# A fused attention and swish kernel: batch 2's queries turned by DMA, two block products alternated, one norm moved

## Chip, cores and metric

The kernel runs on one core of one Trainium2 chip. The metric is the device time of one execution in microseconds (us); lower is better. A change of some 0.2% of it (0.55 us) is about the smallest that the measurement tells from none.

## What is computed

The reference has two stages. The first is an attention without a score matrix: the queries get a softmax over the head's 64 columns, the keys a softmax over the sequence, and each head's 64x64 product of keys and values is applied to the queries. The second is a two-layer network with a swish.

```python
# q, k, v: (batch 8, heads 8, seq 576, dim 64)
q_s = softmax(q, axis=-1)
k_s = softmax(k, axis=2)
kv  = einsum('bhsd,bhse->bhde', k_s, v)
x   = einsum('bhsd,bhde->bhse', q_s, kv)      # then to (4608 tokens, 512)
h   = x @ w_in                                # 512 -> 2048
g   = h / (1 + exp(-beta * h))
out = g @ w_out                               # 2048 -> 512
```

## The kernel before

The 4608 tokens are worked off in nine slabs of 512. Slab t (0 to 7) holds the first 512 rows of batch t's sequence; slab 8 holds the last 64 rows of all eight batches, the "remainder".

**A slab.** Each slab has two passes. Pass 1 forms h transposed, 16 tiles of 128 features by 512 tokens, from WIN and XT (four matmuls of 512 columns a tile, L377). ScalarE applies the swish (L628), VectorE scales by 1/beta (`scale_g`, L651), and the result is GT. Pass 2 multiplies GT by WOUT. In slab 0 it is the plain product (`pass2_group`). In slabs 1 to 8 it is `pass2_fast`, which cuts the product into 2x2 blocks and needs seven block products in place of eight. Each block product is 16 matmuls of 256 columns (L728), eight blocks i for two halves u. The first, into bank s, multiplies GS1 (a sum of two quarters of GT) by WSUM; the second, into bank z5, multiplies GS2 (another sum) by WOUT. The sums are made on VectorE during pass 1, in pieces: blocks 0 to 3, then 4 and 5, then 6, then 7 (L682 `g_sum1`, L687 `g_sum2`). Block 7 can be summed only after the slab's last tile has gone through ScalarE and `scale_g`. When both products are done VectorE copies bank s to TS (L792) and subtracts bank z5 from it (L795), later bank z2 (L801). Bank z5 is then written again by the fourth product. Two differences of GT (`g_diff`, L694) are made on VectorE and used by the last two products.

**Attention.** Batch t+1's attention is laid between the matmuls of slab t and of the next pass 1. ScalarE takes exponentials (L300, and L312 for the key remainder). A norm (`norm_main`) is a sum over 64 columns (L331) and a reciprocal (L332) on VectorE, and a product (L333) on VectorE or POOL, as its last argument says. The normed queries EQ are transposed to QT in one of two ways: on TensorE with an identity (`t_steps`, L375, evacuated to QT at L395), or by a DMA transpose [...], issued from SP (`turn`, L484; `norm_turn` is a norm on POOL and a `turn`). `kv_steps` form keys times values (EK and VB, remainder EKR and VR), VectorE scales and masks them into KVD (L439, L419), and `out_step` multiplies KVD by QT (four per batch, L377) and evacuates to XT (L457). Batches 0, 1 and 2 are transposed on TensorE, batches 3 to 7 by DMA.

**Order.** All order is written by hand. Each engine runs its own list in the order in which the program adds operations, with semaphore waits derived from reads, writes and PSUM banks. In the slabs, `tick` counts matmuls (64 slots for pass 1, 32/56 of a slot for each of the 112 matmuls of pass 2) and releases the items of `todo` when their slot is reached. `hooks` of pass 2 release loads, exponentials, casts and norms at eight points between the products. All loads, stores and DMA transposes of the slabs are issued from SP's queue in program order. Batch b uses buffer b % 2 of QF, KF, VF, EQ and QT.

In slab 1, hook 0 releases the exponentials and V casts of batch 2 and the load of batch 4; hooks 2 and 3 release batch 2's two norms on POOL. `attn_late(2)` places four transposes at a time, then keys times values, then the four `out_step`s. In slab 2, `attn_late(3)` places keys times values at slots 97 to 105 and two `out_step`s at 117 to 120.

Of the kernel before, what the change touches and what calls it, by code (L numbers as in the profile page):

```python
# [154 lines left out]
def bass_efficient_attn_shen__then__act_swish_beta_kernel(  # L155
# [12 lines left out]
    with ExitStack() as es:  # L168
# [340 lines left out]
        def attn_late(b):  # L509
            x = []  # L510
            for hp in range(NHP):
                x += out_step(b, hp, MB, ACTE if hp % 2 else DVE)
            k01, k23 = kv_steps(b, (0, 1)), kv_steps(b, (2, 3))
            if b == 2:
                s = spread(t_steps(b, (0, 1), MB, ACTE), 104, 107) + spread(k01, 107, 110)
                s += spread(k23, 110, 113) + [(113.5, lambda: g_diff(1))] + spread(x[0:2], 114, 116)
                s += spread(t_steps(b, (2, 3), MB, ACTE), 116.5, 119)
                return s + spread(x[2:4], 123, 126)
            if b == 3:
                s = spread(k01, 97, 101) + spread(k23, 101, 105) + [(105, lambda: g_diff(1))]  # L520
                return s + spread(x[0:2], 117, 120)
            s = spread(k01, 92, 96) + spread(k23, 96, 99.8) + [(100, lambda: g_diff(1))]
            return s + spread(x, 107, 123)

        def spread(steps, lo, hi):
            return [(lo + (hi - lo) * k / len(steps), s) for k, s in enumerate(steps)]
# [165 lines left out]
        def g_diff(fh):  # L692
            f, th = NG * fh, 1 - fh
            add(DVE, lambda e: e.tensor_tensor(gv(f, th, NG), gv(f, th, NG), gv(f, 1 - th, NG),  # L694
                                               ALU.subtract),
                r=gk(f, 0, NG) + gk(f, 1, NG), w=gk(f, th, NG), war=True)
# [20 lines left out]
        def pass2_fast(t, tick, hooks):  # L717
            s, z5, z2 = HB[hrot[0] % 3], OB[0], OB[1]
            z2s = (OB[1], MB[0]) if t == NSLAB - 1 else (z2, z2)

            def prod(bk, lhs, lk, rhs, rk, first, end=False):
                two = bk == z2 and z2s[0] != z2s[1]
                for i, u in ([(i, u) for u in range(2) for i in range(NG)] if two and end else
                             [(i, u) for i in range(NG) for u in range(2)]):
                    l, r_ = lhs(i, u), rhs(i)
                    st = first and i == 0 and (u == 0 or two)
                    b_ = z2s[u] if two else bk
                    add(PE, lambda e, l=l, r_=r_, st=st, u=u, i=i, b_=b_: e.matmul(  # L728
                        PS[b_][:, 256 * u:256 * u + 256], l, r_, start=st, stop=end and i == NG - 1,
                        skip_group_check=True),  # L730
                        r=lk(i) + rk(i), w=[("ps", b_)], bank=[b_])
                    tick(32.0 / 56)

            def gt(f0, th):
                return (lambda i, u: GT[:, f0 + i, 256 * th + 128 * u:256 * th + 128 * u + 128],
                        lambda i: [("gt", f0 + i, th)])

            def gs2(th):
                return (lambda i, u: GS2[:, i, 256 * th + 128 * u:256 * th + 128 * u + 128],
                        lambda i: [("gs2", i)])  # L740

            def wo(fh, dh):
                return (lambda i: WOUT[:, NG * fh + i, 256 * dh:256 * dh + 256],
                        lambda i: [("wout", NG * fh + i, dh)])

            def wsum(n):
                return lambda i: WSUM[n][:, i, :], lambda i: [("ws", n, i)]

            def out(th, dh):
                return (O2S[t % 2][:, 2 * th:2 * th + 2, 256 * dh:256 * dh + 256],  # L750
                        [("o2", t % 2, 2 * th + u, dh) for u in range(2)])

            def bank3(bk):
                return PS[bk][:, :].rearrange("p (a b) -> p a b", b=256)

            def halves(bk):
                if bk == z2 and z2s[0] != z2s[1]:
                    return [(z2s[0], 0, 1), (z2s[1], 1, 2)]
                return [(bk, 0, 2)]

            def copy(bk, th, dh, eng):
                o, w = out(th, dh)
                for b_, u0, u1 in halves(bk):
                    add(eng, lambda e, b_=b_, u0=u0, u1=u1: (  # L764
                        e.copy if eng == ACTE else e.tensor_copy)(
                        o[:, u0:u1, :], bank3(b_)[:, u0:u1, :]),
                        r=[("ps", b_)], w=w[u0:u1], bank=[b_])
                if t == 8:
                    store8(th, dh)

            def last(bk, th, dh):
                o, w = out(th, dh)
                ts = TS[:, :].rearrange("p (a b) -> p a b", b=256)
                h = halves(bk)
                for b_, u0, u1 in h:
                    add(DVE, lambda e, b_=b_, u0=u0, u1=u1: e.tensor_tensor(  # L776
                        o[:, u0:u1, :], ts[:, u0:u1, :], bank3(b_)[:, u0:u1, :], ALU.add),
                        r=["ts", ("ps", b_)], w=w[u0:u1], bank=[b_])
                    if t == 8 and len(h) == 2:
                        store8(th, dh, u0)  # L780
                if t == 8 and len(h) == 1:
                    store8(th, dh)

            def at(n):
                for f in hooks.get(n, ()):
                    f()

            at(0)
            prod(s, lambda i, u: GS1[:, i, 128 * u:128 * u + 128], lambda i: [("gs1", i)],
                 *wsum(0), True, True)  # L790
            prod(z5, *gs2(0), *wo(1, 1), True)
            add(DVE, lambda e: e.tensor_copy(TS[:, :], PS[s][:, :]), r=[("ps", s)], w=["ts"],  # L792
                bank=[s])
            at(1)
            add(DVE, lambda e: e.tensor_tensor(TS[:, :], TS[:, :], PS[z5][:, :], ALU.subtract),  # L795
                r=["ts", ("ps", z5)], w=["ts"], bank=[z5])
            at(2)
            prod(z2, *gs2(1), *wo(0, 0), True)
            for b_, u0, u1 in halves(z2):
                c = slice(256 * u0, 256 * u1)  # L800
                add(DVE, lambda e, b_=b_, c=c: e.tensor_tensor(  # L801
                    TS[:, c], TS[:, c], PS[b_][:, c], ALU.subtract),
                    r=["ts", ("ps", b_)], w=["ts"], bank=[b_])
            if t > 3:
                g_diff(0)
                g_diff(1)
            at(3)
            prod(z5, *gt(0, 0), *wo(0, 1), False)
            copy(z5, 0, 1, ACTE)
            at(4)  # L810
            prod(z2, *gt(NG, 1), *wo(1, 0), False)
            copy(z2, 1, 0, ACTE)
            at(5)
            prod(z5, *gt(0, 1), *wsum(1), False, True)
            last(z5, 1, 1)
            at(6)
            prod(z2, *gt(NG, 0), *wsum(2), False, True)
            last(z2, 0, 0)
            at(7)
# [15 lines left out]
        def steps(fn, *a):  # L835
            return lambda: go(fn(*a))

        for t in range(NSLAB):
# [12 lines left out]
                todo += [(2, steps(out_step, 0, 3, HEAD, DVE))]  # L851
            elif t < 4:
                todo = attn_late(t + 1)
                if t == 3:
                    todo += [(1, steps(out_step, 3, 2, MB, ACTE)), (2.5, steps(out_step, 3, 3)),
                             (4, one(norm_turn, 4, 2))]
                if t == 1:
                    todo += [(1, steps(out_step, 1, 2, (3,), ACTE)),
                             (3, steps(kv_steps, 1, (3,), (7,))),
                             (6, steps(out_step, 1, 3, (7,), DVE)),  # L860
                             (6.1, one(w_diff, 0)), (6.2, one(w_diff, 1))]
            elif t < 7:
                todo = attn(t + 1)
                if t > 3:
                    todo += spread(outr_steps(2 * t - 5), *((72, 88), (40, 56), (60, 76))[t - 4])
            elif t == 7:
                todo = spread(outr_steps(1), 32, 48)
# [31 lines left out]
            if t == 0:  # L899
# [6 lines left out]
                w_sum(0, 0, 4)  # L906
                w_sum(2, 0, 4)
                norm_main(1, 0, 1, DVE)
                norm_main(1, 1, 1, POOL)
                cast_vr_s(1)  # L910
                w_sum(0, 4, 4)
                w_sum(2, 4, 4)
# [29 lines left out]
            if t == 1:  # L942
                on(0, exps, 2)
                on(0, casts, 2)
                on(0, load, 4)
                on(2, norm_main, 2, 0, 2, POOL)
                on(3, norm_main, 2, 2, 2, POOL)
                on(3, g_diff, 0)
            elif t == 2:
                on(0, exps, 3)  # L950
                on(2, norm_turn, 3, 0)
# [67 lines left out]
```

The softmax here doesn't subtract the row's maximum and nothing guards it: scores larger than these inputs give would overflow.

## Time and profile before

| | us |
|---|---|
| median of 3 runs (276.8 to 277.07) | 276.98 |
| the profiled execution | 277.22 |
| its span in the profile | 275.2 |
| PE busy / idle in the span | 269.1 / 6.1 |
| VectorE (DVE) busy | 193.8 |
| ScalarE (ACT) busy | 183.1 |
| GpSimd (POOL) busy | 64.0 |
| slab 1, first block matmul to that of slab 2 | 61.20 to 91.11 |
| slab 2, the same | 91.11 to 119.29 |

PE is TensorE's matmul stream and PEld its weight loads, which may run ahead. SPq is SP issuing a DMA. A row of the timeline gives start, duration, engine, line, operation, output and inputs, shape, and a count where neighbours were merged; a bracket at its end gives how long that engine had been idle just before and what ended the idle time. A DMA's landing is counted from its issue. The granted TensorE clock is at full speed through the whole span.

### The profile page before, as it was taken

The numbers are of one execution on the slowest core, as the hardware profiler recorded it, in microseconds if no ns is written. First come the engines' busy times: TensorE is split into PE (matmuls) and PEld (weight loads), VectorE is DVE, ScalarE is ACT, GpSimd is POOL, SyncE is SP. The second block draws the span as 40 slices with busy tenths as digits, with TensorE's granted clock in tenths as the row PEclk, the third lists the DMA queues.
The fourth block names the chain that finished last, engine by engine and source line by source line (L and its number), as shares of the span: only waits on it lengthen the run. The fifth ranks groups of instructions, "written<-read, shape, count | busy, mean of one in ns | idle before, by whom it ended". The sixth has DMA issues, their size and how long they took to land.

```text
span 275.2 us, 4707 instructions
## 1 busy us (share of the span) xinstructions
PE 269.1 (98%) x1841; PEld 167.9 (61%) x1841; DVE 193.8 (70%) x414; ACT 183.1 (67%) x286; POOL 64.0 (23%) x82
## 2 busy tenths in 40 slices
PE   8999999999999999999999999999999999999994
PEld 2544444448754785478656875587558745874583
DVE  4954586787758799878778776978497549625862
ACT  4887558789478966896778937893773477018610
POOL 2780030007421089100810570036000100000000
PEclk9999999999999999999999999999999999999999
DMA  7999999989991029930499999103600130012005
GB/s 215 314 205 207 229 331 349 281 258 376 357 299 60 0 42 289 322 117 0 80 276 292 337 335 194 58 4 76 210 2 0 21 152 0 2 54 99 2 0 153
DMA packets 57254, 45.39 MB, mean 165 GB/s; under 512 B 26497, under 2 KB 56209, under 8 KB 56209
## 3 DMA queue, kind: packets, MB, share of 16 engines
q1 hardware_dynamic: 52368, 40.38, 51.3%
q0 software_dynamic: 4240, 4.19, 9.3%
q10 hardware_dynamic: 624, 0.53, 0.6%
q8 instruction: 14, 0.23, 0.4%
q14 instruction: 8, 0.06, 0.1%
HBM read 36.71 MB, written 9.44 MB: 168 GB/s over the span
## 4 chain that ended last, share of the span: by engine, by line
PE 83%; DMA 8%; POOL 4%; DVE 2%; issue 1%; ACT 0%; SPq 0%; POOLq 0%
PE PS L377 49%; PE PS L728 33%; DMA WOUT<-in_moe_w_out_dram 5%; DMA QF<-in_q_dram 3%; POOL EQ L333 2%; POOL WIN L552 1%; POOL VB L348 1%; PE PS L375 1%; DVE QS L331 1%; POOL VR L362 0%; DVE XT L457 0%; ACT GT L628 0%; DVE EQ L333 0%; DVE QI L332 0%; ACT EQ L300 0%
## 5 line engine op out<-in xcount | busy, mean ns | idle before, releaser
L377 PE MATMUL PS<-XT,WIN 128*128 128x512 bf16 x576 | 131.0, 379 | 0.1
L628 ACT ACTIVATE GT<-PS,BETA 128x512 bf16<-128x512 f32 x144 | 95.2, 690 | 39.5 <-PE PS L377 38.9
L377 PEld LDWEIGHTS PS<-XT,WIN 128*128 128x128 bf16 x576 | 53.6, 98 | 61.1 <-DVE XT L457 0.6
L651 DVE TENSOR_SCALAR GT<-GT,RB 128x512 bf16<-128x512 bf16 x144 | 52.1, 381 | 37.1 <-ACT GT L628 36.4
L333 POOL TENSOR_TENSOR EQ<-EQ,QI 128x1024 bf16<-128x1024 bf16 (+1 forms) x14 | 26.9, 1921 | 66.9 <-DVE QI L332 66.2
L728 PE MATMUL PS<-WOUT,GT 128*128 128x256 bf16 x256 | 33.6, 273 | 0.0
L728 PE MATMUL PS<-WSUM,GT 128*128 128x256 bf16 x256 | 31.9, 273 | 0.1
L728 PE MATMUL PS<-WOUT,GS 128*128 128x256 bf16 x256 | 30.4, 273 | 0.0
L728 PEld LDWEIGHTS PS<-WSUM,GT 128*128 128x128 bf16 x256 | 24.9, 98 | 4.0 <-issue 0.2
L728 PEld LDWEIGHTS PS<-WOUT,GT 128*128 128x128 bf16 x256 | 25.0, 98 | 3.4
L728 PEld LDWEIGHTS PS<-WOUT,GS 128*128 128x128 bf16 x256 | 24.6, 98 | 3.4
L764 ACT COPY O2S<-PS 128x512 f32<-128x512 f32 (+1 forms) x17 | 9.4, 561 | 24.1 <-PE PS L728 22.7
L300 ACT ACTIVATE EQ<-QF 128x512 bf16<-128x512 f32 x32 | 18.0, 621 | 7.2 <-DMA QF<-in_q_dram 7.2
L687 DVE TENSOR_TENSOR GS<-GT 128x512 bf16<-128x512 bf16 (+2 forms) x32 | 21.9, 685 | 0.0
L348 POOL CAST VB<-VF 128x512 bf16<-128x512 f32 x25 | 15.7, 629 | 25.8 <-DVE GS L687 14.8
L377 PE MATMUL PS<-VB,EK 128*128 128x129 bf16 x128 | 20.6, 220 | 0.0
L331 DVE TENSOR_REDUCE QS<-EQ 128x16 f32<-128x1024 bf16 (+1 forms) x20 | 19.8, 991 | 0.8 <-ACT EQ L300 0.8
L694 DVE TENSOR_TENSOR GT<-GT 128x2048 bf16<-128x2048 bf16 x16 | 19.7, 1259 | 0.0
L300 ACT ACTIVATE EK<-KF 128x512 bf16<-128x512 f32 x32 | 18.1, 621 | 0.0
L776 DVE TENSOR_TENSOR O2S<-TS,PS 128x512 f32<-128x512 f32 (+1 forms) x17 | 10.7, 644 | 8.8 <-PE PS L728 8.8
L457 ACT CAST XT<-PS 128x512 bf16<-128x512 f32 x18 | 10.4, 582 | 9.4 <-PE PS L377 9.4
L728 PE MATMUL PS<-WSUM,GS 128*128 128x256 bf16 x128 | 16.4, 273 | 0.0
(78 smaller groups left out, 241.8 us busy)
## 6 DMA issues: line engine op xcount, KB each, us to landing
out_dram<-O2S SPq DMA_DIRECT2D x8, 1024.0 KB, 5.4
QF<-in_q_dram SPq DMA_DIRECT2D x6, 1024.0 KB, 7.5
KF<-in_k_dram SPq DMA_DIRECT2D x6, 1024.0 KB, 9.1
VF<-in_v_dram SPq DMA_DIRECT2D x6, 1024.0 KB, 12.0
KF<-in_k_dram SPq DMA_DIRECT2D x8, 256.0 KB, 5.5
VF<-in_v_dram SPq DMA_DIRECT2D x8, 256.0 KB, 5.5
WOUT<-in_moe_w_out_dram POOLq DMA_DIRECT2D x4, 512.0 KB, 16.4
WIN<-in_moe_w_in_dram POOLq DMA_DIRECT2D x3, 512.0 KB, 9.3
```

The lines of the kernel that those rows point to most:

```text
L300: add(ACTE, lambda e, o=o, a=a: e.activation(o, a, ACT.Exp), r=[(name + "f", i, hp)], w=[("e" + name, i, hp)])
L331: add(DVE, lambda e: e.tensor_reduce(s_, a, AX.X, ALU.add), r=ks, w=[("qs", i, hp0)])
L333: add(eng, lambda e: e.tensor_tensor(a, a, vb, ALU.mult), r=ks + [("qi", i, hp0)], w=ks)
L348: add(eng, lambda e: (e.copy if eng == ACTE else e.tensor_copy)(o, a), r=[("vf", i, hp), ("vone", i)], w=[("vb", i, hp)], after=after)
L377: add(PE, lambda e: e.matmul(o, l, r_, start=start, stop=stop), r=r, w=w, bank=[bk])
L457: add(eng, lambda e: (e.copy if eng == ACTE else e.tensor_copy)(XT[i][:, hp, :], PS[bk][:, :]), r=[("ps", bk)], w=[("xt", i, hp)], bank=[bk])
L628: add(ACTE, lambda e: e.activation(GT[:, f, :], PS[bk][:, :], ACT.Silu, scale=BETA[:, f:f + 1]), r=[("ps", bk), "beta"], w=[("gt", f, 0), ...
L651: add(DVE, lambda e: e.tensor_scalar(GT[:, f, :], GT[:, f, :], RB[:, f:f + 1], None, ALU.mult), r=k + ["rb"], w=k)
L687: add(DVE, lambda e: e.tensor_tensor(GS2[:, i:i + n, :], GT[:, i:i + n, :], GT[:, i + NG:i + NG + n, :], ALU.add), r=[k_ for f in (i, i + ...
L694: add(DVE, lambda e: e.tensor_tensor(gv(f, th, NG), gv(f, th, NG), gv(f, 1 - th, NG), ALU.subtract), r=gk(f, 0, NG) + gk(f, 1, NG), w=gk(f ...
L728: add(PE, lambda e, l=l, r_=r_, st=st, u=u, i=i, b_=b_: e.matmul(PS[b_][:, 256 * u:256 * u + 256], l, r_, start=st, stop=end and i == NG - ...
L776: add(DVE, lambda e, b_=b_, u0=u0, u1=u1: e.tensor_tensor(o[:, u0:u1, :], ts[:, u0:u1, :], bank3(b_)[:, u0:u1, :], ALU.add), r=["ts", ("ps ...
```

## The change

Four edits stand in the diff. The two block products are cut in two: blocks 0 to 5 of the first, blocks 0 to 5 of the second, then blocks 6 and 7 of the first, blocks 6 and 7 of the second (in all of slabs 1 to 8). Batch 2 is treated as batch 3 is: `norm_turn` in place of a norm and `t_steps`, its first two `out_step`s late in slab 1, its last two in pass 1 of slab 2. The load of batch 4 goes from hook 0 of slab 1 to hook 3, behind the two turns on SP's queue. The product of batch 1's second norm goes from POOL to VectorE.

```diff
@@ attn_late @@
-            if b == 2:
-                s = spread(t_steps(b, (0, 1), MB, ACTE), 104, 107) + spread(k01, 107, 110)
-                s += spread(k23, 110, 113) + [(113.5, lambda: g_diff(1))] + spread(x[0:2], 114, 116)
-                s += spread(t_steps(b, (2, 3), MB, ACTE), 116.5, 119)
-                return s + spread(x[2:4], 123, 126)
-            if b == 3:
+            if b < 4:
                 s = spread(k01, 97, 101) + spread(k23, 101, 105) + [(105, lambda: g_diff(1))]
                 return s + spread(x[0:2], 117, 120)
@@ pass2_fast @@
-            def prod(bk, lhs, lk, rhs, rk, first, end=False):
+            def prod(bk, lhs, lk, rhs, rk, first, end=False, part=range(NG)):
                 two = bk == z2 and z2s[0] != z2s[1]
-                for i, u in ([(i, u) for u in range(2) for i in range(NG)] if two and end else
-                             [(i, u) for i in range(NG) for u in range(2)]):
+                for i, u in ([(i, u) for u in range(2) for i in part] if two and end else
+                             [(i, u) for i in part for u in range(2)]):
...
             at(0)
-            prod(s, lambda i, u: GS1[:, i, 128 * u:128 * u + 128], lambda i: [("gs1", i)],
-                 *wsum(0), True, True)
-            prod(z5, *gs2(0), *wo(1, 1), True)
+            def prod_s(part):
+                prod(s, lambda i, u: GS1[:, i, 128 * u:128 * u + 128], lambda i: [("gs1", i)],
+                     *wsum(0), True, True, part)
+
+            prod_s(range(0, 6))
+            prod(z5, *gs2(0), *wo(1, 1), True, False, range(0, 6))
+            prod_s(range(6, NG))
+            prod(z5, *gs2(0), *wo(1, 1), True, False, range(6, NG))
             add(DVE, lambda e: e.tensor_copy(TS[:, :], PS[s][:, :]), r=[("ps", s)], w=["ts"],
                 bank=[s])
@@ the slabs @@
             elif t < 4:
                 todo = attn_late(t + 1)
+                if t > 1:
+                    todo += [(1, steps(out_step, t, 2, MB, ACTE)), (2.5, steps(out_step, t, 3))]
                 if t == 3:
-                    todo += [(1, steps(out_step, 3, 2, MB, ACTE)), (2.5, steps(out_step, 3, 3)),
-                             (4, one(norm_turn, 4, 2))]
+                    todo += [(4, one(norm_turn, 4, 2))]
...
                 norm_main(1, 0, 1, DVE)
-                norm_main(1, 1, 1, POOL)
+                norm_main(1, 1, 1, DVE)
                 cast_vr_s(1)
...
             if t == 1:
                 on(0, exps, 2)
                 on(0, casts, 2)
-                on(0, load, 4)
-                on(2, norm_main, 2, 0, 2, POOL)
-                on(3, norm_main, 2, 2, 2, POOL)
+                on(2, norm_turn, 2, 0)
+                on(3, norm_turn, 2, 2)
                 on(3, g_diff, 0)
+                on(3, load, 4)
```

## The prediction

> **What bounds the kernel now.** I read the page first. TensorE is busy 269.1 of 275.2 us (98%), and the chain of work that ended last is 83% PE. So only two things count: matmul work that disappears, and stretches in which PE waits. The list of waits, cut to PE's weight loads (PEld), says where it waits (columns: total us, times, longest):
>
> ```profile
> PEld PS L728 <- DVE GS L682: 1.7, 7, 0.2
> PEld PS L375 <- POOL EQ L333: 1.4, 2, 1.0
> PEld PS L377 <- ACT QT L395: 0.6, 2, 0.3
> PEld PS L377 <- DMA QT<-EQ: 0.2, 1, 0.2
> ```
>
> Each part of the change has its row. In seven of the eight slabs the block products L728 wait for a block sum GS; in slab 6 they don't, since eight small remainder matmuls stand between the first blocks there. Twice a PE transpose (L375) waits for a norm on POOL. Then the timeline of slab 1 (the first of the eight, t = 1) around its output product; columns are start, duration, engine, operation, count, and in brackets the idle time ahead:
>
> ```profile
> 61.20 2.05 PE L728 MATMUL PS<-WSUM,GS 128*128 128x256 bf16 x16
> 62.51 0.29 DVE L682 TENSOR_TENSOR GS<-GT 128x256 bf16<-128x256 bf16 x1
> 62.85 0.11 PEld L728 LDWEIGHTS PS<-WSUM,GS 128*128 128x128 bf16 x2 [0.25 <-DVE GS L682]
> 63.09 3.66 PE L728 MATMUL PS<-WOUT,GS 128*128 128x256 bf16 x32
> 67.49 4.74 POOL L333 TENSOR_TENSOR EQ<-EQ,QI 128x1024 bf16<-128x1024 bf16 x2
> 69.44 0.11 PEld L375 LDWEIGHTS PS<-IDB,EQ 128*128 128x128 bf16 x2 [0.47 <-POOL EQ L333]
> ```
>
> The reader is to see that the eighth block of the first product is there only at 62.80, while its weights could go at 62.60; and that the first transposes hang on POOL's norm. Next the same place in slab 2, which already has DMA transposes and is my template for slab 1 after the change:
>
> ```profile
> 97.20 4.75 POOL L333 TENSOR_TENSOR EQ<-EQ,QI 128x1024 bf16<-128x1024 bf16 x2 [13.68 <-DVE QI L332]
> 99.13 4.08 SPq L484 DMA_TRANSPOSE QT<-EQ  x2
> 102.54 0.38 PE L377 MATMUL PS<-QT,KVD 128*128 128x512 bf16 x1
> 105.22 0.10 PEld L377 LDWEIGHTS PS<-QT,KVD 128*128 128x128 bf16 x1 [0.19 <-DMA QT<-EQ]
> 105.26 0.38 PE L377 MATMUL PS<-QT,KVD 128*128 128x512 bf16 x1
> ```
>
> Here the second DMA transpose lands just in time: the weights of the third QT product wait 0.19 us for it. Last, the end of slab 0:
>
> ```profile
> 37.36 2.09 DVE L706 TENSOR_TENSOR WSUM<-WOUT 128x1024 bf16<-128x1024 bf16 x2
> 37.60 1.31 POOL L333 TENSOR_TENSOR EQ<-EQ,QI 128x512 bf16<-128x512 bf16 x1 [17.20 <-DVE QI L332]
> 38.96 0.23 PEld L375 LDWEIGHTS PS<-IDB,EQ 128*128 128x128 bf16 x4 [0.98 <-POOL EQ L333]
> 39.38 0.67 DVE L331 TENSOR_REDUCE QS<-EQ 128x8 f32<-128x512 bf16 x1
> 41.07 0.23 PEld L375 LDWEIGHTS PS<-IDB,EQ 128*128 128x128 bf16 x4 [0.48 <-DVE EQ L333]
> ```
>
> **What the Trainium skill says.** (1) "TensorE: Matmul & The Clock Gate", section "Architectural detail": PE may pull weight loads ahead of matmuls in flight. So an idle PEld is not a stopped matmul stream, and the trace agrees: PEld idles 0.25 us, but the first product takes 63.09 - 61.20 = 1.89 us from first matmul to the next product's first, and 16 matmuls at the pace of the next 32 (66.58 - 63.09 = 3.49, 0.109 each) would take 1.745. The stall is 0.145, not 0.25. (2) "SBUF — State Buffer", "Who interferes with whom": a VectorE operation with two SBUF inputs contends with a GpSimd operation that reads SBUF. The trace agrees: the pair of L706 at 37.36 beside POOL's norm takes 2.09 us, the same pair at 32.82 with POOL idle 1.29. (3) "DMA: Bandwidth & Descriptors", "Queues, rings and completion order": each DMA engine consumes a queue's descriptors in ring order. The trace agrees: transposes issued onto a quiet queue land in 3.0 to 3.3 us (99.13: 3.1; the second of that pair 3.2), the one at 109.03 behind three 1 MB loads issued from 103.25 took 7.4, the slowest of all 7.9.
>
> I count from each slab's first block matmul, T0: 61.20, 91.11, 119.29, 148.60, 177.24, 205.51, 232.81, 258.99.
>
> **Part 1, alternation.** No instruction is added or removed. Blocks 6 and 7 of product one now come behind 24 matmuls, 24 x 0.109 = 2.6 us after T0. The last sum (GS1) ends at 62.80 = T0 + 1.6 and the GS2 one at 63.14 = T0 + 1.9; blocks 4 and 5 of GS2, needed at 1.3, ended at 60.28. So the 0.145 goes in each slab that has it. What is late next? Product one now ends four matmuls before product two. VectorE's copy L792 (0.69) starts at about T0 + 3.2, so the subtraction L795 starts at about T0 + 3.9. Before, it started at 94.95 = T0 + 3.84. VectorE does not get earlier, only PE does. PE wants L795's bank again after 48 matmuls, T0 + 5.2, and L795 ends near 4.6: 0.6 to spare. In slabs 3 to 8 nothing on PE follows VectorE closely (the difference g_diff(0) in slab 3 ends at 126.69 = T0 + 7.4, wanted after 80 matmuls and 20 of attention, past 8.7). Gain in slabs 3, 4, 5, 7 and 8: 5 x 0.145 = 0.72. In slab 2 the norm hangs on VectorE behind L795, so the second transpose lands at the same time or 0.05 later, and PE waits for it: gain 0.145 less 0.15 to 0.2, call it 0. Slab 1 is in part 2.
>
> **Part 2, batch 2 by DMA (slab 1).** Removed: 16 PE transposes at about 0.055 us (two of them add 0.11 to the 0.11 of the block matmul beside them: 69.57, 69.79), 0.88 in all; two evacuations of 1.01 on ACT, hidden; and waits of weight loads for the norm, the banks and the evacuation (0.47, 0.16, 0.23, 0.26). The changed order of PE instructions in slab 1 is the same as in slab 2, so I don't add these up: I take slab 2's length, 119.29 - 91.11 = 28.18, in place of slab 1's 91.11 - 61.20 = 29.91, and correct it. Both lengths hold four QT products. Corrections: (a) POOL starts its norms at T0 + 6.29 in slab 1 (it casts V first, to 67.41), at T0 + 6.09 in slab 2; both pairs take the same 4.75. So the second transpose is issued at 72.25 and lands at 75.45 = T0 + 14.25, where slab 2's third QT product ran at 105.26 = T0 + 14.15. That costs 0.1, with the hand-over up to 0.2. (b) ACT's exponential of the K remainder ends at 68.19 = T0 + 7.0; the first remainder matmul, at 98.14 = T0 + 7.03 in slab 2, comes 0.145 earlier now: a wait of about 0.2, which the later wait (a) absorbs. (c) The first transpose is issued at about 69.43, behind the store issued at 58.89 that took 12.0 us, so until 70.9. Quiet, it lands at 72.5; behind that store I allow up to 73. PE wants it at about T0 + 11.45 = 72.65, and the second at least 2.7 us later, 75.35 to 75.7. Again nearly absorbed; I put 0.05 on it. Slab 1 becomes 28.18 + 0.1 to 0.4; I take 28.4. Gain 1.5 (1.3 to 1.65).
>
> The DMA moved too: batch 4's three loads and four remainders stand behind both turns on SP's queue. The first is issued at about 73.6 instead of 65.62. Their issue up to the store's end of landing took 65.62 to 84.8; the same 19 us from 73.6 ends near 92.5. They are needed from 99.43 (ACT's exponential of batch 4), and slab 2's turns come at about 97.5: hidden, by 5 us. Without that cover slab 2 would wait like the 7.4 us case.
>
> **Part 3, batch 1's second norm on VectorE.** POOL's 1.31 becomes 0.69 (the same L333 at 34.98). PE's transposes start at about 38.2 instead of 38.96. But VectorE runs without idle from 36.52 to 42.57: its two L706 now come 0.74 later, at 38.1, and without POOL beside them take 1.29, so the next reduction starts at 39.3 instead of 39.38. PE, after 8 matmuls, waits for that third norm until about 41.0 as before. The stall moves; gain 0 to 0.1. The ends: 0.5 gained (PE's own wait) if the third norm came early enough, 0.7 lost if the L706 stay at 2.09. I take 0.
>
> **Sum.** 1.5 + 0.72 + 0 + 0 = 2.2. Against the profiled run: 277.22 - 2.2 = 275.0. The median of the runs shown is 0.24 below that run, so 276.98 - 2.2 = 274.8.
>
> **Rivals.** (A) The landings don't bind: slab 1 reaches 28.03 (gain 1.88), slab 2 keeps 0.145, slab 0 gives 0.5: with the 0.72, 3.25 in all, 273.7. For it: 0.1 us decides each; against: the 0.19 already waited in slab 2. (B) The alternation's gain is swallowed by VectorE's later subtraction, or the first transpose lands 1 us late behind the store: 0.72 to 1 less, about 275.7. Against the first speaks the 0.6 to spare. (C) Slower: the first turn stands in a full queue. At 7.9 us it lands at 77.3, the first QT product is 4.7 late, the third runs at 80.0 instead of 75.45, and 4.6 lost against 2.2 gained ends at 279.4. It decides from a landing 5.5 us after issue, where the slip reaches 2.2. For it: DMA runs at 350 GB/s until the store lands; against: only 1.5 us of that store is left at 69.4, and the loads now stand behind.
>
> **Chances.** Forecast 0.63 (its own range 274.3 to 275.3), A 0.12, B 0.17, C 0.05, something unseen that leaves it unchanged 0.03. The range 273.7 to 275.8 takes in A and most of B. 0.2% (0.55 us) is about what a measurement can tell from no change.
>
> **What would show it.** The row L728 <- DVE GS gone; first to second product without a gap; slab 1 about 28.4 long, slab 2 28.2, slab 3 29.15; PE waiting for QT's DMA in slabs 1 and 2 by 0.1 to 0.4; L706's second pair at 1.3 and PE's stall in slab 0 now ahead of the third transposes. A QT wait over 1 us in slab 1, a new wait on L795's bank, or a first turn landing after 75 would prove me wrong.

## The result, and the profile after

| | before | changed kernel |
|---|---|---|
| median of 6 runs | 277.01 us | 274.92 us |
| lowest and highest | 276.8, 277.12 | 274.59, 275.83 |
| the profiled execution, its span | 277.22, 275.2 us | 274.92, 273.1 us |

The ratio is 0.9929, with a 95% interval of 0.9914 to 0.9943: 2.1 us, or 0.7%, faster. The forecast was 274.8 us. The sum was nearly met, in part by luck: slabs 0 and 1 gained 0.2 us more than was written for them, and slab 2 lost 0.37. The wider spread (1.24 us between lowest and highest, 0.32 before) was not foreseen at all.

From the list of PE's weight-load waits in the changed kernel (total us, times, longest):

```profile
PEld PS L375 <- DVE EQ L333: 3.0, 6, 1.1
PEld PS L377 <- DMA QT<-EQ: 0.9, 3, 0.5
PEld PS L375 <- POOL EQ L333: 0.6, 1, 0.6
PEld PS L377 <- ACT EKR L312: 0.2, 1, 0.2
PEld PS L377 <- DMA QTR<-EQR: 0.2, 1, 0.2
```

The row of the block products waiting for GS is gone. Of the first row's 3.0 us, 1.6 stand at the end of slab 0; the rest, and the row of POOL, lie in batch 0's attention at the start, whose last transposes come at 12.18 in both kernels. The wait for QT's DMA has grown from 0.2 us once to 0.9 in three places. At the end stands a row that the kernel before did not have: a wait for QTR, the remainder's DMA transpose. It is short in this execution, but the experiments trace most of the spread to it.

I use the prediction's measure: a slab runs from its first block matmul to the next slab's (the last one to the end of the span, which is given to 0.1 us).

| slab | before | changed | gain | forecast gain |
|---|---|---|---|---|
| 0 (start to slab 1) | 61.20 | 61.09 | 0.11 | 0 to 0.1 |
| 1 | 29.91 | 28.29 | 1.62 | 1.5 |
| 2 | 28.18 | 28.55 | -0.37 | 0 |
| 3 | 29.31 | 29.17 | 0.14 | 0.145 |
| 4 | 28.64 | 28.51 | 0.13 | 0.145 |
| 5 | 28.27 | 28.12 | 0.15 | 0.145 |
| 6 | 27.30 | 27.28 | 0.02 | 0 |
| 7 | 26.18 | 26.04 | 0.14 | 0.145 |
| 8 | 16.21 | 16.05 | 0.16 | 0.145 |
| sum | 275.2 | 273.1 | 2.10 | 2.2 |

Slab 1's timeline after, at the places that the prediction showed of it (start, duration, engine, operation, count, idle time ahead):

```profile
61.09 1.47 PE L723 MATMUL PS<-WSUM,GS 128*128 128x256 bf16 x12
62.40 0.29 DVE L677 TENSOR_TENSOR GS<-GT 128x256 bf16<-128x256 bf16 x1
62.40 1.47 PE L723 MATMUL PS<-WOUT,GS 128*128 128x256 bf16 x12
63.71 0.60 PE L723 MATMUL PS<-WSUM,GS 128*128 128x256 bf16 x4
67.39 4.74 POOL L333 TENSOR_TENSOR EQ<-EQ,QI 128x1024 bf16<-128x1024 bf16 x2
69.32 4.07 SPq L484 DMA_TRANSPOSE QT<-EQ  x2
75.34 0.10 PEld L377 LDWEIGHTS PS<-QT,KVD 128*128 128x128 bf16 x1 [0.24 <-DMA QT<-EQ]
```

The last sum is ready at 62.69, and product one comes back to it only at 63.71: no gap. From 61.09 to 63.71 there are 24 matmuls, 0.109 each. The third QT product runs at 75.34, which is 14.25 us after the slab's first block matmul, the place that the prediction gave for it, and it waits for the second turn.

Slab 2's timeline after:

```profile
92.64 0.69 DVE L792 COPY TS<-PS 128x512 f32<-128x512 f32 x1 [1.32 <-PE PS L723]
93.44 0.69 DVE L795 TENSOR_TENSOR TS<-TS,PS 128x512 f32<-128x512 f32 x1
95.69 4.74 POOL L333 TENSOR_TENSOR EQ<-EQ,QI 128x1024 bf16<-128x1024 bf16 x2 [13.91 <-DVE QI L332]
97.61 4.07 SPq L484 DMA_TRANSPOSE QT<-EQ  x2
100.75 0.10 PEld L377 LDWEIGHTS PS<-QT,KVD 128*128 128x128 bf16 x1 [0.20 <-DMA QT<-EQ]
103.89 0.10 PEld L377 LDWEIGHTS PS<-QT,KVD 128*128 128x128 bf16 x1 [0.50 <-DMA QT<-EQ]
```

Counted from the slab's first block matmul at 89.38, VectorE's subtraction L795 starts at 4.06 (3.84 before), POOL's norm at 6.31 (6.09 before), and the third QT product runs at 14.51 (14.15 before). Every step of the chain is late by the same 0.22; the rest is the second turn's landing, 3.4 us after its issue in this execution, 3.2 before.

Slab 0's end after:

```profile
38.05 1.29 DVE L701 TENSOR_TENSOR WSUM<-WOUT 128x1024 bf16<-128x1024 bf16 x2
38.19 0.24 PEld L375 LDWEIGHTS PS<-IDB,EQ 128*128 128x128 bf16 x4 [0.31 <-DVE EQ L333]
39.25 0.68 DVE L331 TENSOR_REDUCE QS<-EQ 128x8 f32<-128x512 bf16 x1
40.95 0.23 PEld L375 LDWEIGHTS PS<-IDB,EQ 128*128 128x128 bf16 x4 [1.12 <-DVE EQ L333]
```

The pair of sums fell from 2.09 to 1.29 us, the second transposes come 0.77 earlier, and the third wait 1.12 instead of 0.48. The stall has moved.

### The profile page after: what moved, and what is told of

Read it like the earlier page. It is cut to its first block, busy times and chain, and to the rows that moved or that the text cites. A ratio compares the mean times of both kernels' runs of the same rounds, so it can differ in the third digit from the quotient of the medians.

```text
span 273.1 us, 4650 instructions
## 1 busy us (share of the span) xinstructions
PE 265.5 (97%) x1802; PEld 167.3 (61%) x1825; DVE 193.3 (71%) x415; ACT 180.7 (66%) x284; POOL 62.2 (23%) x81
## 4 chain that ended last, share of the span: by engine, by line
PE 80%; DMA 9%; DVE 4%; POOL 4%; issue 1%; ACT 0%; SPq 0%; POOLq 0%; DVEq 0%
PE PS L377 47%; PE PS L723 33%; DMA WOUT<-in_moe_w_out_dram 5%; DMA QF<-in_q_dram 3%; POOL EQ L333 2%; POOL WIN L547 1%; DVE QS L331 1%; DMA QT<-EQ 1%; DVE EQ L333 1%; DVE WSUM L701 0%; DVE QI L332 0%; PE PS L375 0%; DVE XT L457 0%; DVE TS L792 0%; DVE TS L795 0%
## 5 line engine op out<-in xcount | busy, mean ns | idle before, releaser
L377 PE MATMUL PS<-XT,WIN 128*128 128x512 bf16 x562 | 129.6, 379 | 0.8
L333 POOL TENSOR_TENSOR EQ<-EQ,QI 128x1024 bf16<-128x1024 bf16 (+1 forms) x13 | 25.6, 1967 | 49.9 <-DVE QI L332 49.2
L723 PE MATMUL PS<-WOUT,GS 128*128 128x256 bf16 x256 | 31.8, 273 | 0.2
L723 PE MATMUL PS<-WSUM,GT 128*128 128x256 bf16 x256 | 30.4, 272 | 0.2
```

The source lines that it names most:

```text
L333: add(eng, lambda e: e.tensor_tensor(a, a, vb, ALU.mult), r=ks + [("qi", i, hp0)], w=ks)
L377: add(PE, lambda e: e.matmul(o, l, r_, start=start, stop=stop), r=r, w=w, bank=[bk])
```

## The experiments

In two questions a theory stood against a rival: why did slab 2 get longer, and where does the spread come from? Times are medians; ratios are against runs of the kernel before on the same chip, with 95% intervals. The kernel before had medians of 277.01 to 277.36 us on the chips used, so kernels that ran on different chips are compared by their ratios. Slab lengths come from the one profiled execution of each kernel.

**Each part alone.** e1 is the kernel before with the two products cut in parts as in the change; e2 has batch 2's turns, placement and load order only; e3 has one line:

```diff
-                norm_main(1, 1, 1, POOL)
+                norm_main(1, 1, 1, DVE)
```

> Part 1 alone on the kernel before. Theory (VectorE's subtraction L795 slips to 4.06 us after the slab's first block matmul because its copy of bank s now ends only after product two, so slab 2's norm, DMA turn and third QT product slip too): slab 2 grows from 28.18 to about 28.5 us, slabs 3, 4, 5, 7, 8 lose 0.13 to 0.16 each, slab 1 0 to 0.15; about 0.4 us faster than the kernel before. Rival (slab 2 grew in the changed kernel because batch 4's load comes later and the DMA queue is fuller): here the load is where it was, so slab 2 keeps 28.0 to 28.2; 0.7 to 0.9 us faster.

> Part 2 alone (batch 2 by DMA, its products placed like batch 3's, batch 4's load behind the turns). Theory: slab 1 shrinks from 29.91 to about 28.3 us, slab 2 stays at 28.2, the rest unchanged; 1.6 us faster than the kernel before. Rival (later load fills the queue): slab 2 grows to about 28.5 and the gain is 1.2 us.

> Part 3 alone. Theory: the pair of WSUM sums falls from 2.09 to 1.3 us, PE's wait moves from the second to the third transposes, the time changes by 0 to 0.1 us. Rivals: the stall vanishes, 0.5 us faster; or VectorE gets longer by the norm, 0.6 us slower.

| | ratio | slab 1 | slab 2 | slab 4 |
|---|---|---|---|---|
| before | 1 | 29.91 | 28.18 | 28.64 |
| e1, alternation | 0.9981 (0.9972 to 0.9989) | 29.93 | 28.37 | 28.50 |
| e2, batch 2 by DMA | 0.9943 (0.993 to 0.9955) | 28.88 | 28.24 | 29.01 |
| e3, norm on VectorE | 0.9998 (0.999 to 1.0006) | 29.89 | 28.18 | 28.64 |
| all three | 0.9929 (0.9914 to 0.9943) | 28.29 | 28.55 | 28.51 |

The alternation alone makes slab 2 longer by 0.19 although the load is where it was, and L795 starts at 4.05 in it. In e2, where the load has moved and the products are whole, L795 starts at 3.83 and slab 2 grows by 0.06 only. So the alternation costs slab 2 time by way of VectorE, and the later load little or nothing. The other 0.1 to 0.2 of the one changed trace was a slow landing: other kernels with the same order in slab 2 gave 28.29 to 28.48. In slab 1 alone the alternation gains nothing: PE then waits 0.62 in place of 0.47 for POOL's norm, which hangs on POOL's casts. e3 changes nothing measurable. The three gains, 0.5, 1.5 and 0.1 us, add up to about the 2.1 of all three.

e2 missed its expectation for slab 1 by 0.6 (28.88 for 28.3; its profiled execution was the slowest of its five). The prediction had named the likely reason: slab 0's store landed at 72.25 in that execution (71.36 in the changed kernel's), the first turn landed 3.9 us after its issue instead of 3.1, and PE's first QT product stood waiting for 0.49 us; e2 also keeps the stall of 0.145 that the alternation takes away.

```profile
73.16 0.10 PEld L377 LDWEIGHTS PS<-QT,KVD 128*128 128x128 bf16 x1 [0.77 <-DMA QT<-EQ]
73.17 0.39 PE L377 MATMUL PS<-QT,KVD 128*128 128x512 bf16 x1 [0.49 <-DMA QT<-EQ]
```

That the store made the turn late rests on few traces: with the store landing at 71.61 (e6) the turn took 3.24 us, and 3.14 to 3.16 in the other kernels with turns at this time and the store ahead of them, where it landed at 71.4 or earlier.

**The load's place.** e4 is the changed kernel with batch 4's load ahead of the turns:

```diff
                 on(0, casts, 2)
+                on(0, load, 4)
                 on(2, norm_turn, 2, 0)
                 on(3, norm_turn, 2, 2)
                 on(3, g_diff, 0)
-                on(3, load, 4)
```

> The changed kernel with batch 4's load put back ahead of batch 2's turns on SP's queue. Theory (SP issues in order, and the load's last issue ended at 78.5 us in the kernel before, so both turns wait for it and for the queue; the first lands at 82 to 86 us instead of 72.4): slab 1 about 10 us longer, 285 us in all. Rival (the place of the load is free, transposes find their way past it): 275 us, as the changed kernel.

It took 288.35 us, ratio 1.038 (1.0361 to 1.04). SP's own list in that kernel, and PE's wait:

```profile
71.71 4.41 SPq L275 DMA_DIRECT2D KRF<-in_k_dram  x2
76.17 2.98 SPq L275 DMA_DIRECT2D VRF<-in_v_dram  x2
79.19 3.64 SPq L484 DMA_TRANSPOSE QT<-EQ  x2
83.52 0.10 PEld L377 LDWEIGHTS PS<-QT,KVD 128*128 128x128 bf16 x1 [11.14 <-DMA QT<-EQ]
```

Both norms were done at 72.1, and the turns were issued from 79.19, when the last load had been issued. Slab 1 took 41.72 us. The load's place on SP's queue is thus what lets the change pay at all: without it a gain of 2.1 us is a loss of 11. That is 3 us more than was expected, because PE's clock fell during the wait (last section).

**VectorE's slip in slab 2.** Two mends of the same step, each on the changed kernel. e5 lets product one end 8 matmuls ahead of product two, not 4; e6 leaves slab 2 alone in the old order:

```diff
-            prod(z5, *gs2(0), *wo(1, 1), True, False, range(0, 6))
+            prod(z5, *gs2(0), *wo(1, 1), True, False, range(0, 4))
             prod_s(range(6, NG))
-            prod(z5, *gs2(0), *wo(1, 1), True, False, range(6, NG))
+            prod(z5, *gs2(0), *wo(1, 1), True, False, range(4, NG))
```

```diff
-            prod_s(range(0, 6))
+            cut = NG if t == 2 else 6
+            prod_s(range(0, cut))
...
```

> The changed kernel with blocks 0 to 3 of product two between the parts of product one, in place of 0 to 5, so that product one ends 8 matmuls before product two and not 4. Theory: block 7 is still ready in time, VectorE's copy L792 is done when product two ends, L795 starts at 3.7 us after the slab's first block matmul instead of 4.06; slab 2 shrinks from 28.55 to about 28.2 us, slab 1 by 0 to 0.1 (POOL's casts bind there); about 0.35 us faster than the changed kernel, 274.5 us. Rival (slab 2 is longer because of a fuller DMA queue): no change against the changed kernel, 274.9 us.

> The changed kernel with slab 2 alone in the old order (product one whole, then product two). Theory: slab 2 goes back to about 28.2 us although it has its stall of 0.145 again, 274.5 us in all. Rival (fuller DMA queue): slab 2 stays at 28.5 or grows to 28.7, 274.9 to 275.1 us.

| | L795 at | POOL's norm at | slab 2 | slab 4 | median | ratio |
|---|---|---|---|---|---|---|
| changed | 4.06 | 6.31 | 28.55 | 28.51 | 274.92 | 0.9929 (0.9914 to 0.9943) |
| e5 | 3.70 | 5.95 | 28.04 | 29.88 | 275.08 | 0.9929 (0.9916 to 0.9942) |
| e6 | 3.83 | 6.09 | 28.29 | 28.57 | 274.71 | 0.9913 (0.99 to 0.9925) |

The timeline of e5 shows the copy done before product two ends, so that L795 now waits for PE and not for the copy:

```profile
92.23 0.69 DVE L792 COPY TS<-PS 128x512 f32<-128x512 f32 x1 [0.88 <-PE PS L723]
93.11 0.69 DVE L795 TENSOR_TENSOR TS<-TS,PS 128x512 f32<-128x512 f32 x1 [0.18 <-PE PS L723]
95.36 4.74 POOL L333 TENSOR_TENSOR EQ<-EQ,QI 128x1024 bf16<-128x1024 bf16 x2 [13.54 <-DVE QI L332]
```

The chain moved as the theory says, and slab 2 with it. One trace of each would not settle slab 2's length, since a landing moves it by 0.1 to 0.3. Over all traces it was 28.29 to 28.55 (mean 28.40) in six kernels with the change's order there, 28.18 to 28.29 (28.22) in four with the old one, and 28.04 to 28.28 (28.18) in three with e5's. e6's time is lower than the changed kernel's, but the intervals overlap. e5's ratio did not fall: in the profiled execution, the slowest of its six, slab 4 took 1.37 us more than the changed kernel's, where nothing else was edited. That was the lead to the spread.

**The third norm's order in slab 0.** e7 puts the two sums behind the norms:

```diff
-                w_sum(0, 4, 4)
-                w_sum(2, 4, 4)
                 norm_main(1, 2, 1, DVE)
                 norm_main(1, 3, 1, DVE)
+                w_sum(0, 4, 4)
+                w_sum(2, 4, 4)
```

> The changed kernel with VectorE's two WSUM sums of slab 0 put behind batch 1's third and fourth norms. Theory (PE's wait for the third norm in slab 0 hangs on VectorE's order, not on the data): the third transposes come 0.6 to 0.9 us earlier and PE's 0.63 us wait goes; 0.3 to 0.6 us faster than the changed kernel. Rival (the loads of batch 1 bind next): the wait moves to the next step, 0 to 0.1 us.

The third transposes came at 39.67, 1.28 us earlier, without a wait. But slab 0's product had begun 0.32 earlier in this execution (28.61 for 28.93), and slab 1 began only 0.08 earlier, at 61.01 against 61.09. The rival held: PE's weight loads next waited 0.87 for POOL's cast of V and 0.77 for the scaling of KVD. POOL itself had waited for V's load, and its cast took 1.14 us where it ran beside VectorE's norm and sums, against 0.61 in the changed kernel. The ratio was 0.9948 (0.9931 to 0.9965), no better than the changed kernel's; slab 4 took 30.02 in this trace. So the stall in slab 0 belongs to a chain of several steps, of which the second norm is one.

**Where slab 4's extra time comes from.** In e5's and e7's traces one PE wait fills it: 1.69 and 1.84 us for the remainder transpose QTR, in slab 5's pass 1 (which lies in slab 4's count). e10 is the changed kernel once more. e8 moves the products that read QTR in slab 5 to later slots, e9 is that with e5's cut:

```diff
-                    todo += spread(outr_steps(2 * t - 5), *((72, 88), (40, 56), (60, 76))[t - 4])
+                    todo += spread(outr_steps(2 * t - 5), *((72, 88), (72, 88), (60, 76))[t - 4])
```

> The changed kernel with one edit: the remainder products of batches 4 and 5 (they read the DMA-transposed QTR) come at slots 72 to 88 of slab 5 in place of 40 to 56, about 7 us later. Theory (a wait on QTR's transpose, behind batch 7's load in the DMA queue, is what now takes 0 to 1.3 us in slab 4's length from run to run, since TensorE has moved up and the queue hasn't): the wait goes, slab 4 is 28.5 us whatever the queue does, the runs lie closer together (274.4 to 275.1 at most) and the median falls by 0.2 to 0.6 us against the changed kernel. Rival (the spread comes from elsewhere, for instance slab 1's first turn): median and spread as the changed kernel's, 274.9 us.

> The same edit together with blocks 0 to 3 of product two between the parts of product one. Theory: slab 2 at 28.0 us (0.5 less than the changed kernel's) and slab 4 at 28.5 us; 274.2 us, the fastest so far. Rival (the earlier slab 2 only makes the next transfer late): 274.7 us or more, with a new wait for a DMA in slabs 3 to 6.

> The changed kernel as it is, beside the next one on the same chip, to see its spread. Theory (the wait on QTR's transpose comes and goes with the DMA queue): runs between 274.5 and 275.9 us, 1 us or more apart, and in the profiled run slab 4 is longer than 28.3 us by just the time that TensorE waits for QTR. Rival (the spread was one odd run): all runs within 0.4 us.

The first line is of e10's waits; the second list shows SP's queue and PE's weight load in it:

```profile
PEld PS L377 <- DMA QTR<-EQR: 1.5, 1, 1.5
```

```profile
151.72 4.53 SPq L268 DMA_DIRECT2D VF<-in_v_dram  x1
156.29 4.43 SPq L275 DMA_DIRECT2D QRF<-in_q_dram  x2
160.76 5.95 SPq L484 DMA_TRANSPOSE QT<-EQ  x2
167.17 1.20 SPq L491 DMA_TRANSPOSE QTR<-EQR  x1
171.33 0.10 PEld L377 LDWEIGHTS PS<-QTR,KVD 128*128 128x128 bf16 x1 [1.51 <-DMA QTR<-EQR]
```

The same transpose in the kernel before:

```profile
161.41 5.75 SPq L484 DMA_TRANSPOSE QT<-EQ  x2
167.20 2.17 SPq L491 DMA_TRANSPOSE QTR<-EQR  x1
```

| | runs | ratio | slabs 4 and 5 together |
|---|---|---|---|
| changed | six, 274.59 to 275.83 | 0.9929 (0.9914 to 0.9943) | 56.63 |
| e10, changed again | six, 275.0 to 276.27 | 0.9929 (0.9914 to 0.9943) | 57.82 |
| e8 | four, 274.62 to 274.86 | 0.9908 (0.9893 to 0.9923) | 56.63 |
| e9 | four, 274.5 to 274.77 | 0.9907 (0.989 to 0.9923) | 56.62 |

The transpose stands behind batch 7's load and two turns, and from 148 to 161 the DMA engines move 315 GB/s before and 327 after. It was issued at 167.17 in e10 and at 167.20 before, and in five traces of kernels with the change and the reader at its old place at 166.1 to 167.3: it moved up by at most 1.1 us, while PE moved up by 1.8 to 2.2 at this place. Before, it landed at 170.6 and PE asked for it at 171.62, one microsecond to spare. In those five traces PE asked at 169.4 to 169.9 and it landed at 169.9 to 171.4, so that PE's weight load waited 0.15 to 1.84. The margin was thin already: in e3, where PE has not moved, it landed at 171.5, and PE waited 0.2.

With the reader 7 us later the spread is 0.24 us in four runs of e8, 0.27 in e9 and 0.33 in e11 below, in place of 1.24 and 1.27 in six of the changed kernel, and slabs 4 and 5 lose nothing by it. The wait for QTR is thus shown as the main source of the change's spread. It is not all there is: the kernel before itself spread over 0.26 to 0.82 us on the other chips (7 to 24 runs). That e8's time is lower too is likely but not separated, since its interval overlaps the changed kernel's. e9 did not show e5's shorter slab 2 again (28.28): its first turn landed 3.6 us after issue, and PE waited for that one instead.

**A version that takes these together.** e11 is e9 with slab 0's store behind batch 2's turns:

```diff
-                    if n == 10:
-                        store(0)
...
                 on(3, g_diff, 0)
+                on(3, store, 0)
                 on(3, load, 4)
```

> The changed kernel with the late remainder products, blocks 0 to 3 between the parts, and slab 0's store (1 MB) issued behind batch 2's two turns and ahead of batch 4's load. Theory: the first turn of batch 2 meets an empty queue and lands 3.0 to 3.2 us after its issue in every run; slab 1 at 28.2 to 28.3 us, nothing else moves; 274.3 to 274.7 us with runs within 0.4 us. Rival (the store and the load, later by 3 us, collide with slab 2's turns): slab 2 above 28.6 us, 275 us or more.

274.42 us (274.27 to 274.6), ratio 0.9893 (0.988 to 0.9906), beside 275.30 for the changed kernel on the same chip, whose ratio is 0.9929 (0.9914 to 0.9943): the intervals do not meet, and its ratio is the lowest of all. The first turn landed 3.1 us after issue, as it also did in the changed kernel's trace; slab 1 took 28.23 and slab 2 28.22 us. Which of its three edits brings how much was not separated further, and that the store's new place gains anything is not shown.

## Why the prediction held, point by point

**The place of the bound.** Right. PE stayed the chain, and the gain came from PE's waits and from dropped transposes.

**The size of the alternation's stall.** Right: 0.145 per slab from the matmul stream, not the 0.25 of the weight loads. Slabs 3, 4, 5, 7 and 8 gave about 0.7 together, as forecast; the eight small matmuls in slab 6 did cover it there (0.02).

**Slab 1 by analogy with slab 2.** Right in mechanism and nearly in size: 28.29 for 28.4, gain 1.62 for 1.5. Correction (a), POOL's later norm, was the whole of it; the third QT product stands at 14.25 as written. Corrections (b) and (c) were absorbed: the wait for EKR is there with 0.22 us. But (c), the store ahead of the first turn, was priced at 0.05, and in e2's execution PE stood 0.49 us for that turn.

**Slab 2 kept at 0.** Wrong in size. The failing step is "so the subtraction L795 starts at about T0 + 3.9", followed by "lands at the same time or 0.05 later". The copy started at T0 + 3.26, not 3.2, and from its start to the subtraction's start 0.80 us passed, not 0.69: the subtraction needs the copy's result, and 0.11 us lay between them. So L795 started at 4.06, 0.22 later than before, and slab 2 lost 0.11 to 0.37 in six traces instead of nothing. In slab 2 the change's order is a loss, as e6 shows by taking it back (28.22 on average with the old order, 28.40 with the change's). e5 shows that it is the short lead of product one that costs, and not the alternation as such.

**Part 3.** Right: nothing gained, with the times of each step met within 0.1 us (38.19, 1.29, 39.25, 40.95 for 38.2, 1.29, 39.3, 41.0). The 0.11 gained in slab 0 is mostly not its doing: slab 0's product already began 0.09 earlier, at 28.93 for 29.02.

**The load behind the turns.** Right: its tail, slab 1's store, landed at 91.6 (issued at 85.97, 92.5 forecast), 6 us ahead of slab 2's turns.

**The rivals.** None of A, B and C came: slab 1 kept the wait that A left out, no wait for L795's bank is in the list, and the first turn landed 3.1 us after its issue. C was right that the queue ahead of the first turn decides. It had priced a slow landing; e4 shows a case that it did not describe, with the turns not issued before the load, and 13 us lost against the changed kernel.

**What was not considered.** That PE moving up by nearly 2 us makes it wait for a transfer three slabs on, whose time is set by the DMA queue. The prediction's look at the queue stopped at slab 2. Both sets of runs of the changed kernel have it, one of six runs over 275.5 us in the first and two of six over 276 in the second, at the same ratio of 0.9929 (the second chip is the slower one, with 277.36 for 277.01 before). So the forecast's hit does not show that this term was nothing.

## What to carry to other kernels

When PE is moved up, list every transfer whose time is set by other transfers and not by PE, in all later stages, and compare its landing with the new time of its reader; here two later slots for the reader took the spread from 1.2 us to 0.3 or less. When two products feed one chain on another engine, let the first one end early enough for its follow-up to be done when the second ends, as in e5. And a transpose by DMA was cheap here only with little ahead of it on its queue: look at what the issuing engine still has to issue before it.

## What the runs showed of the hardware

In e4 PE stood idle for 11 us, and the granted TensorE clock fell with it. Busy time by stretch (PE, PEld, DVE, ACT, POOL; then the clock, the DMA share and GB/s):

```profile
72.00:74.00 2.00, 0.66 (x7) 0.35 (x4) 1.17 (x1) 0.00 (x0) 0.09 (x1) 1.00 1.08 348
74.00:75.00 1.00, 0.00 (x0) 0.00 (x0) 0.00 (x0) 0.00 (x0) 0.00 (x0) 0.99 1.10 351
75.00:76.00 1.00, 0.00 (x0) 0.00 (x0) 0.00 (x0) 0.00 (x0) 0.00 (x0) 0.50 1.10 347
87.00:88.00 1.00, 1.00 (x7) 0.69 (x6) 0.00 (x0) 0.00 (x0) 0.00 (x0) 0.50 0.00 0
88.00:89.00 1.00, 1.00 (x6) 0.58 (x5) 0.35 (x1) 0.00 (x0) 0.00 (x0) 0.68 0.00 0
89.00:90.00 1.00, 1.00 (x6) 0.45 (x5) 0.53 (x2) 0.82 (x2) 0.00 (x0) 1.00 0.00 0
```

PE's last matmul ended at 72.7, the clock fell to half at about 75.0, and it came back at about 88.6, 5.1 us after PE had work again at 83.5. PE's matmuls had stood for 10.9 us, and 5.1 us at half the clock cost about 2.6 more: together 13.5, and slab 1 was 13.4 us longer than in the changed kernel. The Trainium skill, "TensorE: Matmul & The Clock Gate", section "What's actually happening", tells of half the clock after at least one idle window of about 3.4 us, and of full clock after at least one busy one. The trace agrees on the half; the times differ, with a fall after 2.3 us without a matmul and a recovery of 5.1 us, and why is not settled here. Waits of up to 1.84 us of the weight loads (1.34 of the matmuls, in e7) left the clock at 1.
